# Decoded magnitudes kept in PSUM, and the second unit's key products and inverse started earlier, in a delta-rule attention and mixture-of-experts kernel

## The chip, the cores and the metric

The kernel runs on one core of a Trainium2 chip. The metric is the device time of one execution in microseconds, as the median of several runs. The engines are called by the names of the profile: PE (TensorE, matrix products), PEld (its weight loads), DVE (VectorE), ACT (ScalarE), POOL (GpSimd) and SP (SyncE, which issues most DMAs). All of them run in parallel, each through its own queue in order.

## The reference

Three parts follow one another. The change touches the first part and the preparation of the second.

```python
# 1: delta-rule attention, q, k, v of (4, 8, 768, 48), one state of 48 x 48 for each of 32 heads
k_n = k / (norm(k) + 1e-6)
for t in range(768):
    y[t] = q[t] @ state
    state = state + beta[t] * outer(k_n[t], v[t] - k_n[t] @ state)
# 2: x of (3072, 384) = the heads of y side by side; weights in float64
x = (((x @ w1) * (x @ w2)) @ w3) @ w_out
# 3: each of 3072 tokens goes through one of 8 experts, chosen by x @ w_gate + bias
out = gate * (relu(x @ e_w1[e]) @ e_w2[e])
```

## The kernel before

**Attention.** The 768 steps are cut into 12 chunks of 64 (`s`), and two chunks make a unit (`u`). Within a chunk the recursion is replaced by products with the inverse of a triangular matrix. For a unit, `gram` multiplies the keys with themselves on PE (four calls of 8 head pairs) and ACT copies the negated result from PSUM into `An`, one full copy and two small ones that bring the lower diagonal blocks of 32 together. `inverse` is a generator: it transposes these blocks so that all 32 x 128 small matrices lie across partitions (`Ab`), takes the norms from their diagonals (square root on ACT, then about ten short DVE operations), scales `Ab` by beta and the norms, runs 31 rows of a recursion (two DVE operations each, `tmp` and `Tt`), multiplies with beta and transposes back (`An`, `TT`). Each `next` on the generator is one step. `merge1` and `merge2` join the blocks of 32 to 64 (products `pe`, `pf`, copies on ACT). Then follows the chain of a chunk: `chain_k` (values scaled with the norms by `scaled`, on POOL, less what the state says), `chain_u` (product with the inverse, `pu`), `chain_y` (the output, `py`, put by DMA into the token layout `x`), `chain_s` (the new state, `pS`). `masked` multiplies queries with keys.

**Start-up.** `startup` reads the float64 weights as raw words, 36 tiles in the order of `todo`: 8 tiles of w_out (384 columns), 16 of w3 and 12 of w1 and w2 (512 columns). A tile is decoded by two ACT operations, the magnitude (`mag`) and the low part, and two DVE operations that join them. Raw tiles go to ten buffers; `mag` alternates between two buffers in SBUF, which lie with the tenth raw buffer in the tile `spare` under the name `An1`. `sc`, in the place of the second unit's `TT`, takes the decoded tile. w_out is transposed and multiplied with the gate weights (`wot`, `wog`); w3 is folded with w_out on PE (`pw`) and split into two parts (`w34h`, `w34l`); w1 and w2 are only split (`w`).

**Order.** The wrapper `Engine` records each operation and makes every engine execute in the order of the program text, so all lines of the profile are its line 84, and groups are told apart by tile names. The order in start-up is written out by hand: `tick(n)` issues ACT's decode of tile n + 1, DVE's of tile n, what has become due (`flush`), new raw loads, and PE's use of tile n; the table `do` hangs other work behind a tick. `FC` is 8, so `FC + 3` is tick 11. In `do` stand the steps of the first inverse (`EARLY`, `START0`: four steps behind each of ticks 8 to 15), the chain of chunk 0 (from tick 17, one function for each tick), the key products of unit 1 (`GRAMS`, ticks 19 to 22), the routing set-up and the first steps of the second inverse (`WORK1`, ticks 30 to 33). After tick 33 the first token block follows: `moe1` runs 12 blocks of 256 tokens with 8 slices `f` each; a slice multiplies with w1 and w2 (`pAB`, two PSUM buffers of the name `AB`), DVE forms the product `a`, ACT and DVE split it (`ch`, `cl`), and `second` multiplies with the folded weights (`px`). `slot` places the attention of the following chunk between the slices, and `PLAN1` says how many steps of the second inverse the first block takes behind each slice. Tiles 34 and 35 are decoded within slices 0 and 1 of the first block (`rest`).

Of the kernel before, what the change touches and what calls it, by code (L numbers as in the profile page):

```python
# [53 lines left out]
MID = (0,) * 5 + (0, 0, 1) + (2, 2, 2, 1, 1, 1, 1, 2)  # L54
PLAN1 = (3, 4, 4, 4, 5, 4, 4, 2)
WORK1 = (1, 1, 1, 1)
AHEAD, W0 = 8, 0
CHAIN, GRAMS = (1, 1, 1, 1, 1, 1), (2, 3, 4, 5)
START0 = (4, 4, 4, 4, 4, 4, 4, 4, 2)

REST = (1, 1)
EARLY = (4, 2)
LEAD = 1
# [40 lines left out]
class Kernel:  # L104
# [162 lines left out]

    def keys(self, u):

        nc, a2 = self.nc, self.a2  # L270
        kT = a2.tile([P, NU, C], F32, tag="kT", name="kT")
        for c in range(US):
            nc.sync.dma_start(out=kT[:, c * NP:(c + 1) * NP].rearrange("p n t -> p (n t)"), in_=self.k_t[u * US + c])
        bt = a2.tile([P, 32], F32, tag="bt", name="bt")
        nc.sync.dma_start(out=bt, in_=self.beta[u])
        self.st[u] = dict(kT=kT, bt=bt)
# [10 lines left out]
    def gram(self, u, a):  # L287

        nc, a1, ps = self.nc, self.a1, self.ps
        st = self.st[u]
        if "An" not in st:
            st["An"] = a1.tile([P, NU, C], F32, tag=f"An{(u + 1) % 2 if u else 0}", name="An")
        An, kT = st["An"], st["kT"]
        pg = ps.tile([P, HP, C], F32, tag="ps", name="pg")
        for n in range(HP):
            for h in range(2):
                o, w = (1 - h) * C, h * C  # L300
                nc.tensor.matmul(pg[o:o + C, n], kT[w:w + C, a + n], kT[w:w + C, a + n], start=True, stop=True)
        yield
        nc.scalar.activation(An[:, a:a + HP], pg, AF.Copy, scale=-1.0)

        for h in range(2):
            o = h * C + 32
            nc.scalar.activation(An[o:o + 32, a:a + HP, 0:32], pg[o:o + 32, :, 32:64], AF.Copy, scale=-1.0)
# [9 lines left out]
    def scaled(self, s):  # L317
        u, c = divmod(s, US)
        vt = self.st["v", s]
        self.nc.gpsimd.tensor_tensor(out=vt, in0=vt, in1=self.st[u]["r"][:, c * NP:(c + 1) * NP].unsqueeze(2).to_broadcast([P, NP, D]), op=ALU.mult)  # L320

    def inverse(self, u):
# [6 lines left out]
        nc.gpsimd.memset(T, 0.0)  # L329
        nc.gpsimd.memset(T.rearrange("p a b -> p (a b)")[:, 0:1024:33], 1.0)  # L330
        nc.vector.transpose(Ab.rearrange("n j i -> n i j"), An[:, :, 0:32].rearrange("j n i -> j i n"))

        ss, r, r2, rb = (a2.tile([P, 32], F32, tag=x, name=x) for x in ("ss", "r", "r2", "rb"))
        nc.vector.tensor_scalar(out=ss, in0=Ab.rearrange("p a b -> p (a b)")[:, 0:1024:33], scalar1=-1.0, scalar2=0.0, op0=ALU.mult, op1=ALU.max)
        nc.scalar.activation(r, ss, AF.Sqrt)
        yield
# [10 lines left out]
        st["r"] = rb  # L347
        nc.vector.tensor_tensor(out=Ab, in0=Ab, in1=bt.unsqueeze(2).to_broadcast([P, 32, 32]), op=ALU.mult)
        yield
        tmp = a1.tile([P, 256], F32, tag="tmp", name="tmp")  # L350
        for j in range(31):
# [5 lines left out]
            yield  # L357
        nc.vector.tensor_tensor(out=T, in0=T, in1=bt.unsqueeze(1).to_broadcast([P, 32, 32]), op=ALU.mult)

        nc.vector.transpose(An[:, :, 0:32].rearrange("i n c -> i c n"), T)  # L360
# [161 lines left out]
    def startup(self):  # L522
# [3 lines left out]
        nc, pm, wp, m1 = self.nc, self.pm, self.wp, self.m1  # L526
        self.keys(0)

        self.w12 = [[[[None] * KC for _ in range(2)] for _ in range(2)] for _ in range(2)]
# [3 lines left out]
        sc = self.TT[1].rearrange("p n c -> p (n c)").rearrange("p (a b) -> p a b", b=DCH)  # L533
        spare = self.a1.tile([P, 4, DCH], F32, tag="An1", name="spare")
        ms = [spare[:, x] for x in range(2)]
        wg = self.cp.tile([P, KC, E], F32, tag="wg", name="wg")
# [18 lines left out]
        def issue():  # L555
            while issued[0] < len(todo):
                n = issued[0]
# [12 lines left out]
                if kind != "o":  # L570
                    out[n] = sc[:, n % 4]
                mag[n] = ms[n % 2][:, :src.shape[-1]]
                tag = usable[0]
                free.remove(tag)
                k = src.shape[-1]
                t = spare[:, 2:4].rearrange("p a b -> p (a b)")[:, 0:2 * k].bitcast(I64) if tag == "raw" else (wp if tag[0] == "w" else m1).tile([P, k], I64, tag=tag, name="raw")
                nc.sync.dma_start(out=t, in_=src)
# [3 lines left out]
        def scalar(n):  # L581

            if n < len(todo):
                L, Hw, _ = raw[n]

                nc.scalar.activation(mag[n], Hw.bitcast(F32), AF.Abs, scale=2.0 ** -112)
# [58 lines left out]
        def tick(n):  # L645
            self.n = n
            scalar(n + 1)
            vector(n)
# [4 lines left out]
        def split(g):  # L653

            next(g)
            after.append((self.n + 1, lambda: list(g)))

        inv = self.inverse(0)
        prep = lambda a: self.prep(0, [a * HP])
        step = lambda: next(inv, None)  # L660
        do = {-1: [lambda: prep(0), lambda: prep(1), lambda: scalar(0), lambda: prep(2), lambda: prep(3)], 1: [step],
              FC - 4: [lambda: self.queries(0), lambda: self.values(0), self.routing_loads], 
              FC + 3: [lambda: split(self.masked(0))], FC + 5: [lambda: self.tokens(0), lambda: self.keys(1), lambda: self.values(1)]}

        for x in EARLY:
            do.setdefault(FC - x, []).append(step)
        GAPS = list(CHAIN)
# [8 lines left out]
        for x in range(0, NU, HP):  # L676
            do.setdefault(FC + len(START0) + GRAMS[x // HP], []).append(lambda x=x: split(self.gram(1, x)))
        do.setdefault(t, []).append(lambda: setattr(self, "work", self.inverse(1)))
        for n, k in enumerate(WORK1, NSTART - len(WORK1)):
            do.setdefault(n, []).extend([lambda: next(self.work)] * k)  # L680
# [5 lines left out]
        issue()  # L686
        nc.sync.dma_start(out=wg, in_=self.w_gate.rearrange("(k p) e -> p k e", p=P))
        for n in range(-1, NSTART):
# [122 lines left out]
    def routing_setup(self):  # L811
# [526 lines left out]
```

## Time and profile before

| | us |
|---|---|
| median of 3 runs | 858.41 (857.83 to 858.80) |
| the profiled execution | 855.77 |
| its span, first to last instruction | 854.0 |
| PE busy | 796.9 (93%) |
| DVE busy | 613.7 (72%) |
| ACT busy | 409.6 (48%) |
| POOL busy | 162.7 (19%) |

The busy shares are means over the whole span. The start-up and the first token block, which the change rearranges, take the first 196 us or so and have limits of their own; they are read from windows and from the timeline. In a row of the timeline stand the start, the duration, the engine, the line, the operation, the tile that is written and those that are read, how many instructions were merged, and in brackets how long the engine had been idle and what ended that.

### The profile page before, as it was taken

Reading aid. Unit: us, or ns where it says so; the run is one execution under the profiler, and the core shown is the slowest. Engines: PE = TensorE matmul, PEld = TensorE weight load, DVE = VectorE, ACT = ScalarE, POOL = GpSimd, SP = SyncE. Lnnn points to the kernel's source line nnn. Section 1 sums busy time; section 2 is a strip of 40 time slices with the busy share of each in tenths; the row PEclk is TensorE's granted clock in tenths of the full one; section 3 lists DMA queues with packets and bytes.
Section 4 is the critical chain, followed back from the end, with each engine's and each line's share of the span. In section 5 each row is a group of like instructions: output and inputs, shape, how many; then the busy total and the mean of one; then the engine's idle time right before and its main releaser. Section 6 shows DMA issues by size and latency. Waiting matters only on the chain.

```text
span 854.0 us, 24817 instructions
## 1 busy us (share of the span) xinstructions
PE 796.9 (93%) x10223; PEld 739.6 (87%) x10223; DVE 613.7 (72%) x1512; ACT 409.6 (48%) x863; POOL 162.7 (19%) x174
## 2 busy tenths in 40 slices
PE   3977879989999999999999999999899999999994
PEld 3844638988999999999999999999899999999983
DVE  3897399969866986698669874457786678667651
ACT  6525964462445344624462444335555565655541
POOL 5000300010001000100010000003244564545420
PEclk8588979999999999999999999999999999999998
DMA  9835434303220322032202121028457768667620
GB/s 301 289 102 186 126 98 135 83 17 85 71 82 6 98 71 83 21 87 80 68 26 78 39 64 40 2 90 264 128 157 247 243 229 267 227 211 249 223 63 6
DMA packets 48777, 105.42 MB, mean 123 GB/s; under 512 B 9412, under 2 KB 28756, under 8 KB 48656
## 3 DMA queue, kind: packets, MB, share of 16 engines
q1 hardware_dynamic: 41424, 88.35, 33.5%
q0 software_dynamic: 4064, 11.06, 3.8%
q10 hardware_dynamic: 3168, 4.34, 1.4%
q8 instruction: 82, 1.34, 0.7%
q14 instruction: 39, 0.32, 0.1%
HBM read 89.15 MB, written 10.63 MB: 117 GB/s over the span
## 4 chain that ended last, share of the span: by engine, by line
PE 62%; DVE 8%; issue 8%; POOL 4%; ACT 1%; DMA 1%; SPq 0%; POOLq 0%; ACTq 0%; DVEq 0%
PE pAB L84 23%; PE px L84 14%; PE ph L84 7%; PE spy L84 4%; PE py L84 2%; PE pq L84 2%; PE pk L84 2%; PE pu L84 2%; PE pS L84 2%; POOL w1l L84 2%; PE pg L84 1%; PE pe L84 1%; DVE Tt L84 1%; POOL out_dram L84 1%; DVE tmp L84 1%
## 5 line engine op out<-in xcount | busy, mean ns | idle before, releaser
L84 PE MATMUL pAB<-x,w 128*128 128x256 f32 x1728 | 231.3, 288 | 0.0
L84 PEld LDWEIGHTS pAB<-x,w 128*128 128x128 f32 x1728 | 214.6, 192 | 4.1
L84 ACT CAST ch<-a 128x256 fp32r<-128x256 f32 x96 | 38.9, 406 | 117.7 <-DVE a L84 117.7
L84 ACT COPY a<-pAB 128x256 f32<-128x256 f32 x96 | 35.7, 372 | 124.5 <-PE pAB L84 118.4
L84 DVE TENSOR_TENSOR a<-a,pAB 128x256 f32<-128x256 f32 x96 | 39.9, 416 | 73.6 <-ACT a L84 73.4
L84 PE MATMUL ph<-sxh,w1h 128*128 128x256 f32 x288 | 82.1, 285 | 0.5 <-DVE hl L84 0.5
L84 PE MATMUL ph<-sxh,w1l 128*128 128x256 f32 x288 | 80.8, 281 | 0.0
L84 PE MATMUL ph<-sxl,w1h 128*128 128x256 f32 x288 | 80.8, 280 | 0.0
L84 ACT ACTIVATE hh<-ph 128x256 fp32r<-128x256 f32 x96 | 37.0, 385 | 89.1 <-PE ph L84 88.7
L84 DVE TENSOR_TENSOR Tt<-tmp,Tt 128x31 f32<-128x31 f32 (+15 forms) x186 | 63.8, 343 | 6.6 <-DVE tmp L84 0.2
L84 DVE SCALAR_TENSOR_TENSOR hl<-ph,hh 128x256 fp32r<-128x256 f32 x96 | 40.2, 419 | 39.0 <-ACT hh L84 37.7
L84 DVE TENSOR_TENSOR w2l<-r,w2h 128x768 fp32r<-128x768 f32 x56 | 59.3, 1071 | 12.3 <-ACT w2h L84 12.1
L84 DVE TENSOR_TENSOR tmp<-Ab,Tt 128x31 f32<-128x31 f32 (+15 forms) x186 | 65.4, 352 | 3.2
L84 PE MATMUL px<-w34h,ch 128*128 128x392 f32 x192 | 65.8, 343 | 0.8 <-DVE w34l L84 0.8
L84 PE MATMUL px<-w34h,cl 128*128 128x392 f32 x192 | 65.3, 340 | 0.0
L84 PE MATMUL px<-w34l,ch 128*128 128x392 f32 x192 | 65.2, 339 | 0.0
L84 POOL TENSOR_TENSOR w1l<-r,w1h 128x512 fp32r<-128x512 f32 x39 | 50.5, 1313 | 50.4 <-ACT w1h L84 50.2
L84 POOL TENSOR_TENSOR vt<-vt,rb 128x768 f32<-128x768 f32 x12 | 18.2, 1519 | 201.6 <-DMA vt<-in_v_dram 117.7
L84 PEld LDWEIGHTS ph<-sxh,w1h 128*128 128x128 f32 x288 | 54.3, 188 | 1.3 <-DVE hl L84 1.1
L84 PE MATMUL pw<-wosW,TT 128*128 128x392 f32 x80 | 37.0, 605 | 19.5 <-DVE TT L84 19.2
L84 DVE TENSOR_TENSOR cl<-a,ch 128x256 fp32r<-128x256 f32 x96 | 40.4, 421 | 19.6 <-ACT ch L84 18.8
L84 PEld LDWEIGHTS ph<-sxh,w1l 128*128 128x128 f32 x288 | 54.3, 189 | 0.0
(262 smaller groups left out, 1742.9 us busy)
## 6 DMA issues: line engine op xcount, KB each, us to landing
r<-in_e_w_dram SPq DMA_DIRECT2D x42, 512.0 KB, 4.7
r<-in_e_w_dram SPq DMA_DIRECT2D x56, 384.0 KB, 3.9
raw<-in_w_dram SPq DMA_DIRECT2D x25, 512.0 KB, 4.8
kT<-in_kt_dram SPq DMA_DIRECT2D x12, 512.0 KB, 4.1
W<-in_q_dram SPq DMA_DIRECT2D x24, 256.0 KB, 4.4
vt<-in_v_dram SPq DMA_DIRECT2D x12, 384.0 KB, 4.6
kb<-in_kb_dram SPq DMA_DIRECT2D x12, 384.0 KB, 3.5
x2d<-xr ACTq DMA_DIRECT2D x22, 192.5 KB, 3.0
```

Source lines behind the costliest of these rows:

```text
L84: x = f(*a, **kw)
```

## The change

The magnitudes move from SBUF to PSUM: for tiles 0 to 9 to the buffers of the name `pc`, for tiles 10 to 34 to the two of the name `AB`, for tile 35 to a quarter of `sc`. The tile `spare` and with it the tenth raw buffer are gone, and `An1` is free for the second unit. The key products of unit 0 go to four PSUM buffers, all ahead of the first tile; their full copies run on DVE behind ticks 0 to 2, the small ones stay on ACT. The first w_out tile is loaded between the two halves of the first keys, the second behind them, and the gate weights follow. The steps of the first inverse begin behind tick 2 and end behind tick 14, where they ended behind tick 16; the chain begins behind tick 15, where it began behind tick 17. Beta is put on the diagonal of T at the outset, so the product of T with beta at the end falls away. The keys of unit 1 are loaded behind tick 6 instead of 13, their products run behind ticks 9, 10, 12 and 13, and 16 steps of the second inverse behind ticks 16 to 21; the first block takes the other 21. The first two units have one more step, since the square root is a step of its own. The first values are scaled on DVE. The routing set-up moves from ticks 9 to 11 behind ticks 16 to 18, with its PSUM tile in `ps`. Of the tiles of w1 and w2, one now follows each of the last eight tiles of w3, and four come last.

```diff
-PLAN1 = (3, 4, 4, 4, 5, 4, 4, 2)
-WORK1 = (1, 1, 1, 1)
+PLAN1 = (3, 4, 4, 3, 3, 2, 1, 1)
+WORK1 = {0: 2, 1: 2, 2: 3, 3: 3, 4: 3, 5: 3}
-CHAIN, GRAMS = (1, 1, 1, 1, 1, 1), (2, 3, 4, 5)
-START0 = (4, 4, 4, 4, 4, 4, 4, 4, 2)
+CHAIN, GRAMS = (1, 1, 1, 1, 1, 1), (-6, -5, -3, -2)
+START0 = (3, 3, 3, 3, 3, 3, 3)
-EARLY = (4, 2)
+EARLY = {2: 1, 3: 1, 4: 2, 5: 4, 6: 4, 7: 4}
...
     def keys(self, u, also=lambda: None):
             nc.sync.dma_start(out=kT[:, c * NP:(c + 1) * NP]..., in_=self.k_t[u * US + c])
+            if c == 0:
+                also()
...
     def gram(self, u, a):
-            st["An"] = a1.tile([P, NU, C], F32, tag=f"An{(u + 1) % 2 if u else 0}", name="An")
+            st["An"] = a1.tile([P, NU, C], F32, tag=f"An{u % 2}", name="An")
-        pg = ps.tile([P, HP, C], F32, tag="ps", name="pg")
+        own = {2: "x0", 3: "AB"}.get(a // HP) if u == 0 else None
+        pg = self.pm.tile([P, HP, C], F32, tag=own, ...) if own else ps.tile([P, HP, C], F32, tag="ps", name="pg")
...
-        nc.scalar.activation(An[:, a:a + HP], pg, AF.Copy, scale=-1.0)
+        if u == 0:
+            nc.vector.tensor_scalar(out=An[:, a:a + HP], in0=pg, scalar1=-1.0, scalar2=None, op0=ALU.mult)
+        else:
+            nc.scalar.activation(An[:, a:a + HP], pg, AF.Copy, scale=-1.0)
...
     def scaled(self, s):
-        self.nc.gpsimd.tensor_tensor(out=vt, in0=vt, in1=..., op=ALU.mult)
+        (self.nc.gpsimd if s else self.nc.vector).tensor_tensor(out=vt, in0=vt, in1=..., op=ALU.mult)
...
     def inverse(self, u):
-        nc.gpsimd.memset(T.rearrange("p a b -> p (a b)")[:, 0:1024:33], 1.0)
...
+        if u < 2:
+            yield
         nc.scalar.activation(r, ss, AF.Sqrt)
...
-        nc.vector.tensor_tensor(out=Ab, in0=Ab, in1=bt.unsqueeze(2).to_broadcast([P, 32, 32]), op=ALU.mult)
+        nc.vector.tensor_tensor(out=Ab, in0=Ab, in1=bt.unsqueeze(1).to_broadcast([P, 32, 32]), op=ALU.mult)
+        nc.vector.tensor_copy(T.rearrange("p a b -> p (a b)")[:, 0:1024:33], bt)
...
-        nc.vector.tensor_tensor(out=T, in0=T, in1=bt.unsqueeze(1).to_broadcast([P, 32, 32]), op=ALU.mult)
...
     def startup(self):
-            k = (x + 1 - AHEAD) * (len(w12) - sum(REST)) // (K3 - AHEAD)
+            k = x + 1 - AHEAD
-        free = [f"w{m}1{kk}" for kk in range(KC) for m in range(2)] + ["x0", "x1", "xr", "raw"]
+        free = [f"w{m}1{kk}" for kk in range(KC) for m in range(2)] + ["x0", "x1", "xr"]
...
+                if n < FC + 2:
+                    mag[n] = self.pc.tile([P, DCH], F32, tag="pc", name="mag")
+                elif n <= NSTART:
+                    mag[n] = pm.tile([P, DCH], F32, tag="AB", name="mag", bufs=2)
+                else:
+                    mag[n] = sc[:, (n + 2) % 4]
...
         def tick(n):
+            if n >= NSTART:
+                flush(n)
...
+        self.keys(0, lambda: issue(1))
+        issue(2)
+        nc.sync.dma_start(out=wg, ...)
+        issue()
+        grams = [self.gram(0, a) for a in range(0, NU, HP)]
+        for g in grams:
+            next(g)
+        do = {-1: [lambda: scalar(0)], 0: [lambda: list(grams[0])], 1: [lambda: list(grams[1]), lambda: list(grams[2])], 2: [lambda: list(grams[3])],
+              FC - 2: [lambda: self.keys(1)], ...
-        do.setdefault(t, []).append(lambda: setattr(self, "work", self.inverse(1)))
-        for n, k in enumerate(WORK1, NSTART - len(WORK1)):
+        c = FC + len(START0)
+        do.setdefault(c + 1, []).append(lambda: setattr(self, "work", self.inverse(1)))
+        for n, k in WORK1.items():
...
-            do.setdefault(FC + 1 + x, []).append(lambda: next(rs, None))
+            do.setdefault(FC + 8 + x, []).append(lambda: next(rs, None))
...
-        pmod = self.pm.tile([P, NTILE], F32, tag="AB", name="pmod", bufs=2)
+        pmod = self.ps.tile([P, NTILE], F32, tag="ps", name="pmod")
```

## Rows read from the trace of the kernel before

**Rows 1.** Windows: busy us of PE, PEld, DVE, ACT, POOL; PEclk, DMA, GB/s

```profile
0.00:15.60 15.60, 7.22 (x131) 6.88 (x131) 2.14 (x4) 9.71 (x20) 12.61 (x33) 0.95 0.88 297
15.60:74.30 58.70, 44.22 (x198) 30.33 (x198) 54.13 (x120) 23.15 (x47) 1.84 (x1) 0.72 0.67 216
74.30:110.00 35.70, 27.42 (x609) 20.46 (x610) 17.71 (x29) 31.99 (x59) 6.56 (x11) 0.90 0.40 116
110.00:130.00 20.00, 17.05 (x102) 9.62 (x101) 18.96 (x36) 12.29 (x23) 0.00 (x0) 0.84 0.44 136
130.00:196.00 66.00, 61.48 (x1106) 57.83 (x1105) 56.45 (x137) 32.95 (x69) 6.03 (x6) 0.97 0.24 67
```

**Rows 2.** Timeline of DVE: the first transpose

```profile
15.61 2.10 DVE L84 STREAM_TRANSPOSE Ab<-An 128x1024 f32<-128x1024 f32 x1
```

**Rows 3.** Timeline of DVE and POOL from 33 to 75 us

```profile
33.55 2.56 DVE L84 SCALAR_TENSOR_TENSOR TT<-spare,TT 128x512 int32<-128x512 int32 x2
...
33.73 1.84 POOL L84 TENSOR_TENSOR vt<-vt,rb 128x768 f32<-128x768 f32 x1 [19.73 <-DVE Tt L84]
...
69.59 1.23 DVE L84 TENSOR_TENSOR Tt<-Tt,bt 128x1024 f32<-128x1024 f32 x1
...
74.34 0.66 DVE L84 SCALAR_TENSOR_TENSOR TT<-spare,TT 128x512 int32<-128x512 int32 x1
```

**Rows 4.** Windows of DVE alone: norm and scaling, twelve recursion rows, routing

```profile
21.50:24.80 3.30, 3.06 (x11) 0.50 1.03 407
31.30:33.50 2.20, 1.96 (x9) 0.50 1.02 325
36.00:38.90 2.90, 2.66 (x9) 0.50 0.83 299
40.40:43.78 3.38, 3.14 (x9) 0.86 0.50 153
49.10:50.53 1.43, 1.33 (x7) 1.00 0.00 0
```

**Rows 5.** Timeline: ACT, copies of a key product; DVE, tiles 25, 30, 33

```profile
104.16 1.39 ACT L84 ACTIVATE An<-pg 128x512 f32<-128x512 f32 x3
...
107.94 0.68 DVE L84 SCALAR_TENSOR_TENSOR TT<-spare,TT 128x512 int32<-128x512 int32 x1
...
117.72 0.68 DVE L84 SCALAR_TENSOR_TENSOR TT<-spare,TT 128x512 int32<-128x512 int32 x1
...
129.17 0.68 DVE L84 SCALAR_TENSOR_TENSOR TT<-spare,TT 128x512 int32<-128x512 int32 x1
```

**Rows 6.** Timeline of PE, first block; last a window with the clock

```profile
129.27 4.58 PE L84 MATMUL pAB<-x,w 128*128 128x256 f32 x36
...
175.28 2.21 PE L84 MATMUL pe<-An 32*32 32x32 f32 x128 [2.55 <-DVE An L84]
...
177.42 3.86 PE L84 MATMUL pAB<-x,w 128*128 128x256 f32 x18
...
179.50:181.20 1.70, 1.70 (x10) 1.70 (x9) 0.00 (x0) 1.68 (x2) 1.64 (x3) 0.50 0.00 0
```

**Rows 7.** Groups of instructions: busy us, mean ns of one, idle before

```profile
L84 ACT ACTIVATE spare<-raw 128x512 f32<-128x512 f32 x18 | 12.2, 678 | 17.9 <-issue 9.0 <-DVE TT L84 8.8
...
L84 ACT ACTIVATE An<-pg 32x256 f32<-32x256 f32 x16 | 6.0, 376 | 0.3
...
L84 ACT ACTIVATE An<-pg 128x512 f32<-128x512 f32 x8 | 4.8, 600 | 4.9 <-PE pg L84 4.8
...
L84 DVE SCALAR_TENSOR_TENSOR hl<-ph,hh 128x256 fp32r<-128x256 f32 x96 | 40.2, 419 | 39.0 <-ACT hh L84 37.7
...
L84 DVE TENSOR_TENSOR cl<-a,ch 128x256 fp32r<-128x256 f32 x96 | 40.4, 421 | 19.6 <-ACT ch L84 18.8
```

**Rows 8.** DMA issues: count, KB each, median us to landing

```profile
raw<-in_w_dram SPq DMA_DIRECT2D x25, 512.0 KB, 4.8
```

More of the change, by code (lines that the diff above doesn't have):

```diff
@@ L266, in attn_setup, with keys @@
         self.wos = ((big.rearrange("p (g n) -> p g n", n=XW), 5), (R, 1), (K, 1), (one, 1))
-    def keys(self, u):
+    def keys(self, u, also=lambda: None):
         nc, a2 = self.nc, self.a2
@@ L294, in gram @@
         if "An" not in st:
-            st["An"] = a1.tile([P, NU, C], F32, tag=f"An{(u + 1) % 2 if u else 0}", name="An")
+            st["An"] = a1.tile([P, NU, C], F32, tag=f"An{u % 2}", name="An")
         An, kT = st["An"], st["kT"]
-        pg = ps.tile([P, HP, C], F32, tag="ps", name="pg")
+        own = {2: "x0", 3: "AB"}.get(a // HP) if u == 0 else None
+        pg = self.pm.tile([P, HP, C], F32, tag=own, name="pg", bufs=2 if own == "AB" else 1) if own else ps.tile([P, HP, C], F32, tag="ps", name="pg")
         for n in range(HP):
@@ L319, in scaled @@
         vt = self.st["v", s]
-        self.nc.gpsimd.tensor_tensor(out=vt, in0=vt, in1=self.st[u]["r"][:, c * NP:(c + 1) * NP].unsqueeze(2).to_broadcast([P, NP, D]), op=ALU.mult)
+        (self.nc.gpsimd if s else self.nc.vector).tensor_tensor(out=vt, in0=vt, in1=self.st[u]["r"][:, c * NP:(c + 1) * NP].unsqueeze(2).to_broadcast([P, NP, D]), op=ALU.mult)
     def inverse(self, u):
@@ L526, in startup @@
         nc, pm, wp, m1 = self.nc, self.pm, self.wp, self.m1
-        self.keys(0)
         self.w12 = [[[[None] * KC for _ in range(2)] for _ in range(2)] for _ in range(2)]
@@ L533, in startup @@
         sc = self.TT[1].rearrange("p n c -> p (n c)").rearrange("p (a b) -> p a b", b=DCH)
-        spare = self.a1.tile([P, 4, DCH], F32, tag="An1", name="spare")
-        ms = [spare[:, x] for x in range(2)]
         wg = self.cp.tile([P, KC, E], F32, tag="wg", name="wg")
@@ L549, in startup, with issue @@
         last = {f"w{m}1{kk}": todo.index(("w", (m, 1, kk))) for kk in range(KC) for m in range(2)}
-        free = [f"w{m}1{kk}" for kk in range(KC) for m in range(2)] + ["x0", "x1", "xr", "raw"]
+        free = [f"w{m}1{kk}" for kk in range(KC) for m in range(2)] + ["x0", "x1", "xr"]
         raw, out, mag, after = {}, {}, {}, []
         issued = [0]
-        def issue():
-            while issued[0] < len(todo):
+        def issue(upto=100):
+            while issued[0] < min(upto, len(todo)):
                 n = issued[0]
@@ L571, in issue @@
                     out[n] = sc[:, n % 4]
-                mag[n] = ms[n % 2][:, :src.shape[-1]]
                 tag = usable[0]
@@ L575, in issue @@
                 k = src.shape[-1]
-                t = spare[:, 2:4].rearrange("p a b -> p (a b)")[:, 0:2 * k].bitcast(I64) if tag == "raw" else (wp if tag[0] == "w" else m1).tile([P, k], I64, tag=tag, name="raw")
+                t = (wp if tag[0] == "w" else m1).tile([P, k], I64, tag=tag, name="raw")
                 nc.sync.dma_start(out=t, in_=src)
@@ L584, in scalar @@
                 L, Hw, _ = raw[n]
+                if n < FC + 2:
[4 more added lines that the diff above has]
+                    mag[n] = sc[:, (n + 2) % 4]
+                mag[n] = mag[n][:, :L.shape[-1]]
                 nc.scalar.activation(mag[n], Hw.bitcast(F32), AF.Abs, scale=2.0 ** -112)
@@ L656, in split @@
             after.append((self.n + 1, lambda: list(g)))
+        self.keys(0, lambda: issue(1))
+        issue(2)
+        nc.sync.dma_start(out=wg, in_=self.w_gate.rearrange("(k p) e -> p k e", p=P))
+        issue()
         inv = self.inverse(0)
@@ L660, in startup @@
         step = lambda: next(inv, None)
-        do = {-1: [lambda: prep(0), lambda: prep(1), lambda: scalar(0), lambda: prep(2), lambda: prep(3)], 1: [step],
+        grams = [self.gram(0, a) for a in range(0, NU, HP)]
+        for g in grams:
+            next(g)
+        do = {-1: [lambda: scalar(0)], 0: [lambda: list(grams[0])], 1: [lambda: list(grams[1]), lambda: list(grams[2])], 2: [lambda: list(grams[3])],
               FC - 4: [lambda: self.queries(0), lambda: self.values(0), self.routing_loads],
-              FC + 3: [lambda: split(self.masked(0))], FC + 5: [lambda: self.tokens(0), lambda: self.keys(1), lambda: self.values(1)]}
-        for x in EARLY:
-            do.setdefault(FC - x, []).append(step)
+              FC - 2: [lambda: self.keys(1)],
+              FC + 3: [lambda: split(self.masked(0))], FC + 5: [lambda: self.tokens(0), lambda: self.values(1)]}
+        for x, k in EARLY.items():
+            do.setdefault(x, []).extend([step] * k)
         GAPS = list(CHAIN)
@@ L677, in startup @@
             do.setdefault(FC + len(START0) + GRAMS[x // HP], []).append(lambda x=x: split(self.gram(1, x)))
-        do.setdefault(t, []).append(lambda: setattr(self, "work", self.inverse(1)))
-        for n, k in enumerate(WORK1, NSTART - len(WORK1)):
-            do.setdefault(n, []).extend([lambda: next(self.work)] * k)
+        c = FC + len(START0)
+        do.setdefault(c + 1, []).append(lambda: setattr(self, "work", self.inverse(1)))
+        for n, k in WORK1.items():
+            do.setdefault(c + 1 + n, []).extend([lambda: next(self.work)] * k)
         rs = self.routing_setup()
         for x in range(3):
-            do.setdefault(FC + 1 + x, []).append(lambda: next(rs, None))
+            do.setdefault(FC + 8 + x, []).append(lambda: next(rs, None))
         do.setdefault(t + 3, []).append(lambda: self.parts_x(0))
         do.setdefault(NSTART - 1, []).extend([lambda: self.tokens(1), lambda: self.tokens(2)])
-        issue()
-        nc.sync.dma_start(out=wg, in_=self.w_gate.rearrange("(k p) e -> p k e", p=P))
         for n in range(-1, NSTART):
```

## The prediction

> **What bounds the kernel now.** I read the stages first, from the table of windows [rows 1]. Five stretches matter, and what stands in front of each number is which engine is nearly full. Up to 15.6 us VectorE (DVE) is busy 2.14 us: it waits for the first tile. From 15.6 to 74.3 us it is busy 54.1 of 58.7 us, so DVE is the bound: it decodes tiles 0 to 15 and runs the first unit's inverse. From 74.3 to 110 us ScalarE (ACT) is busy 32.0 of 35.7 us and DVE only 17.7: here the first chunk's chain (merge, u, y, state) passes from TensorE (PE) to ACT and back, ACT also decodes and copies the second unit's key products, and 18 us of DVE lie idle. From 110 to 130 us DVE is full again (19.0 of 20). From 130 to 196 us, the first token block, PE is busy 61.5 of 66 us and DVE 56.5: PE is the bound, and it loses 4.5 us to DVE. After that PE is the bound to the far end and the change touches little. So the change is worth what it takes out of the DVE-bound stretches, and what it puts into the 18 idle us without lengthening the chain. I follow four marks: DVE's start of tile 16, of tile 22 and of tile 33, and PE's second product of the first block.
>
> **Up to tile 16 (before: 74.34 us [rows 3]).** Key products of unit 0 now go to four PSUM buffers at once; their large copies move from ACT to DVE. The trace has no such copy on DVE; a DVE operation of 512 columns takes 0.68 us [rows 5], the same copy on ACT 0.60 [rows 7], so 0.6 to 0.7 each, 2.8 us for four, all in a stretch where DVE is idle for 13 of 15.6 us. ACT is rid of four copies of 0.6 us before the first transpose, and the first w_out tile is asked for ahead of the second half of the keys, at some 1.2 us; with a landing like the median of the big loads, 4.8 us [rows 8], it is there at 6. From then ACT's queue up to the transpose holds four tiles (two operations of 384 columns each, 0.55 by columns from the 0.678 for 512 [rows 7]), eight small copies of 0.376 [rows 7] and one of about 0.5: 7.9 us. With some 1.2 us of waits on DVE between, I put the transpose at 15.1 us against 15.61 [rows 2], but with tile 2 already decoded (1.2, two DVE operations of 384 columns). Gain 1.7.
> The product with beta over the whole T (1.23 us [rows 3]) goes; in its place comes a copy of 32 columns, 0.25 with its gap. Gain 1.0. The scaling of the first values leaves POOL: beside its 1.84 us two decode operations took 2.56 us instead of 1.36 [rows 3, 5]. Gain 1.2. [...] The routing set-up, 1.4 us of DVE [rows 4], is only moved behind tile 16: 1.5 here, given back below. DVE idles 4.6 us in this stretch [rows 1]; 1.6 of it are single waits on ACT early on, which a DVE with more to do per tile does not have. Sum: 1.7 + 1.0 + 1.2 + 1.5 + 1.6 = 7.0, so tile 16 starts at about **67.3 us**.
>
> **Magnitudes in PSUM** change no count. That ACT writes PSUM is not in the trace; its magnitude costs 0.678 us from SBUF to SBUF, a copy of as many columns out of PSUM 0.600 [rows 7], so I bound it by 0.08 either way, 34 times: up to 2.7 us, of ACT, which has slack except beside the chain; I take 0. For DVE, the operation hl, with one operand in PSUM, took 0.419 us and cl, with both in SBUF, 0.421 [rows 7]: no price, and I take 0. [...] One raw buffer fewer: loads run 9 tiles ahead, not 10, and tiles 34 and 35 are asked for only after tiles 30 and 31. Four tiles at the pace below are 7.8 us and a load lands in 4.8 [rows 8], so I take 0; if loads crowd and land twice as late, tile 34 is 1.8 us late, the upper end. The second keys move ahead on SP's queue, to tile 6: the raw loads behind them are late by their 1 MB, some 3 us at the 300 GB/s of the first stretch [rows 1], against a lead of 8 tiles; nothing.
>
> **Tile 16 to tile 22.** This is where the idle DVE is used. Its work now: six tiles at 1.35, 8.1 (two operations each [rows 5]); two low parts of w1/w2 and one of the fold, 1.7; the routing, 1.5; the scaling of the first values, by columns from the 1.23 us for 1024 [rows 3], 0.95; and 16 steps of the second inverse: transpose and norm input 2.3 [rows 2], norm and scaling 3.3, and 13 rows of the recursion, the first 0.4 and the next twelve 2.2 + 2.9 + 3.4 = 8.5 [rows 4], in all 14.7 with the diagonal. Together 27.0. The key products of unit 1 (four times 1.39 us of ACT [rows 5]) are out of this stretch, beside the fold, where ACT is busy 23 of 58.7 us [rows 1]. Chain and DVE run side by side, with one wait that I can place: in tile 18 the low part of a w1 tile waits for ACT's high part, which stands behind the copies of the second merge on ACT's queue, about 2.9 us. So tile 22 starts near 67.3 + 27.0 + 2.9 = **97.2**, with 14.7 us of the second inverse behind it.
>
> **Tile 22 to tile 33 (before: 129.17 [rows 5]).** No inverse step and no key product is left here. The pace of such tiles stands in the trace: from 107.94 (tile 25) to 117.72 us five tiles with their splits, 1.96 each [rows 5]. (Tile 25, at 107.94 before, comes near 103.) Eleven make 21.5; POOL's scaling of the second values now falls on a busy DVE, 1.2 as above. Tile 33 starts at **119.9**, 9.3 earlier.
>
> **The first block.** The last two PSUM magnitudes sit in the two buffers of pAB. The first product waits for tile 33, which is about done. The second waits for DVE to read tile 34's magnitude, and before that DVE has tile 33 (1.35), two low parts (1.3), R (1.1), a, a row of the recursion and cl (0.4 + 0.9 + 0.4), a fold part (0.5) and the read itself (0.7): 6.6, so 126.5. Queued behind it on PE are u, the masked queries and every later product. Before, the second product began at 129.27 + 2.29 = 131.56 [rows 6]. Lead **5.1**. From here PE is the bound. It lost 4.5 us [rows 1], of which 2.55 were one wait for the second inverse [rows 6], which now ends inside the block; 0.9 belong to the routing and stay. Gain 3.6. After that wait one product took 3.86 us instead of 2.29, with the granted clock at 0.50, the lower of its two levels [rows 6]; this goes (1.5), but PE now idles some 4 us ahead of the second product and should pay the same there. Sum: 5.1 + 3.6 = **8.7 us**. The profiled execution (855.8 us, span 854.0) would become 847.1; it lies 2.6 below the median of the runs, 858.4, so I forecast 849.7.
>
> **Rivals.** *More is saved (845.3).* If DVE does not stand still in tile 18 (2.9) and PE's clock holds through the short wait (1.5), the gain is 8.7 + 4.4 = 13.1. For it: ACT loses 5.6 us of work there; against it: 32.0 of 35.7 us.
> *PSUM reads are dear (852.4).* If a decode operation on DVE pays for PSUM the 0.08 us by which ACT's two rows differ, the only gap between the memories that the rows show [rows 7], 34 tiles cost 2.7 us, all in stretches that DVE bounds: 8.7 less 2.7 is 6.0. Against it: hl and cl. [...]
> *The work only moves (857.4).* If idle DVE time is not filled but displaced, what is left is what DVE no longer does: twice 1.0 and the 1.2 of the collision, less 0.95 for the scaling and 1.2 for the new collision, 1.0 in all. Against it: the 18 us are idle because ACT and PE are the bound there.
> *The chain is strung out (slower, 861.7).* Each tile's chain step on PE stands behind that tile's fold, which needs DVE; DVE's next split needs ACT; ACT's copies need PE. If, instead of running side by side, the 14.7 us of inverse between tiles 16 and 22 are met by such waits one after another, most of them, 12 us, come on top of the 8.7 saved: 3.3 slower. It decides against the change from the point where tile 22 starts later than about 106 us.
>
> **How the numbers follow.** Forecast, 846 to 853: 0.60. More saved: 0.14. PSUM dear: 0.10. Only moved: 0.08. Strung out: 0.08. Range 844.5 to 856: it takes in the first three with their bounds and leaves out the last two. A difference of 0.2% (1.7 us) is about what a measurement of this kernel can tell from none. Faster 0.84, same 0.08, slower 0.08.
>
> **What will show it.** In the new trace: the transpose of unit 0 near 15 us; tile 16 near 67 and the first merge's products near 71; tile 22 near 97 with the twelfth row of the second recursion done; DVE idle between 74 and 110 us down from 18 to under 6; decode operations still 0.68; the second pAB product behind a wait of 3 to 4 us; no wait of 2.55 before the second unit's merge. I am wrong if a decode operation takes over 0.72 us, if tile 22 begins after 100, or if PE's wait before the second product exceeds 6 us.

## The result, and the profile after

The changed kernel takes **849.51 us** (median; 848.02 to 850.87) against 858.12 (857.06 to 858.80) for the kernel before in the same comparison: a ratio of 0.990, 95% interval 0.9881 to 0.992, or 8.6 us less. The forecast was 849.7. The profiled execution of the changed kernel took 850.87 us, its span 849.2.

The same five windows as [rows 1], now of the changed kernel (us, busy PE, PEld, DVE, ACT, POOL, then granted clock, DMA share, GB/s):

```profile
0.00:15.60 15.60, 7.49 (x141) 7.19 (x142) 5.95 (x11) 8.98 (x19) 10.76 (x22) 1.00 0.89 284
15.60:74.30 58.70, 48.95 (x453) 33.94 (x452) 52.92 (x116) 31.87 (x64) 2.42 (x11) 0.80 0.62 210
74.30:110.00 35.70, 24.24 (x353) 15.75 (x352) 31.72 (x71) 22.30 (x42) 5.51 (x9) 0.81 0.42 130
110.00:130.00 20.00, 15.99 (x122) 10.97 (x121) 18.34 (x32) 14.55 (x28) 0.00 (x0) 0.96 0.63 175
130.00:196.00 66.00, 65.11 (x1238) 61.48 (x1237) 49.50 (x129) 32.41 (x67) 5.83 (x5) 0.99 0.21 61
```

DVE works 3.8 us more ahead of 15.6 us. Between 74.3 and 110 it idles 4.0 us where it idled 18.0. Between 130 and 196 PE loses 0.9 us where it lost 4.5, but its wait of 2.6 us ahead of the second product now lies before 130. The marks on DVE, from its timeline, with POOL's scaling of the second values, which answer to [rows 2, 3, 5]:

```profile
15.31 2.13 DVE L84 STREAM_TRANSPOSE Ab<-An 128x1024 f32<-128x1024 f32 x1 [1.59 <-ACT An L84]
...
69.62 0.57 DVE L84 TENSOR_TENSOR w34l<-pw,w34h 128x392 fp32r<-128x392 f32 x1 [2.76 <-ACT w34h L84]
70.10 0.68 DVE L84 SCALAR_TENSOR_TENSOR TT<-mag,TT 128x512 int32<-128x512 int32 x1
...
92.62 0.69 DVE L84 TENSOR_TENSOR w<-TT,w 128x512 fp32r<-128x512 f32 x1 [2.04 <-ACT w L84]
...
96.88 2.27 DVE L84 TENSOR_TENSOR tmp<-Ab,Tt 128x231 f32<-128x231 f32 x1
97.39 1.49 POOL L84 TENSOR_TENSOR vt<-vt,rb 128x768 f32<-128x768 f32 x1
99.18 0.40 DVE L84 TENSOR_TENSOR Tt<-tmp,Tt 128x231 f32<-128x231 f32 x1
...
101.28 0.68 DVE L84 SCALAR_TENSOR_TENSOR TT<-mag,TT 128x512 int32<-128x512 int32 x1
...
121.87 0.69 DVE L84 SCALAR_TENSOR_TENSOR TT<-mag,TT 128x512 int32<-128x512 int32 x1
```

Tile 16 starts at 70.10 us (before 74.34), tile 22 at 101.28, tile 33 at 121.87 (before 129.17). On PE the first products and the second unit's merge, which answer to [rows 6]:

```profile
122.70 2.39 PE L84 MATMUL pAB<-x,w 128*128 128x256 f32 x18
127.71 3.59 PE L84 MATMUL pAB<-x,w 128*128 128x256 f32 x18 [2.62 <-DVE a L84]
...
168.52 2.21 PE L84 MATMUL pe<-An 32*32 32x32 f32 x128
170.67 2.42 PE L84 MATMUL pAB<-x,w 128*128 128x256 f32 x18
```

The window of the second pAB product, with the clock:

```profile
127.70:131.20 3.50, 3.49 (x18) 3.29 (x18) 3.36 (x8) 1.56 (x3) 0.00 (x0) 0.61 1.02 226
```

The lead over before is 3.85 us at the second pAB product (131.56 before), 6.8 at `pe`, with no wait ahead of it, and 8.2 at the routing product `pr` (187.74 against 195.97). There it stays until some 600 us. Two later marks on PE, `spt`, first of the changed kernel, then of the kernel before:

```profile
600.07 0.44 PE L84 MATMUL spt<-ident,xg 128*128 128x128 f32 x2 [1.15 <-DVE sxl L84]
...
662.95 0.38 PE L84 MATMUL spt<-ident,xg 128*128 128x128 f32 x2
```
```profile
608.05 0.44 PE L84 MATMUL spt<-ident,xg 128*128 128x128 f32 x2 [1.15 <-DVE sxl L84]
...
667.88 0.38 PE L84 MATMUL spt<-ident,xg 128*128 128x128 f32 x2
```

At the first the lead is 8.0 us, at the second 4.9, and the two profiled spans differ by 4.8. So the missing 3 us lie between these marks, in the clock: PE does the same work there in 59.0 busy us after the change, at a mean clock of 0.95, and in 56.1 before, at 1.00, and idles 3.9 and 3.7 us. First a window of the changed kernel, then of the kernel before:

```profile
600.00:620.00 20.00, 17.93 (x114) 17.63 (x115) 15.47 (x44) 6.92 (x15) 4.24 (x5) 0.91 0.52 163
```
```profile
600.00:620.00 20.00, 16.39 (x121) 15.78 (x119) 15.80 (x45) 10.67 (x26) 5.50 (x6) 1.00 0.46 129
```

The changed kernel's clock drops to 0.50 twice (from 606.4 to 609.6 us and from 640.6 to 643.8), that of the kernel before stays at 1.00. Of the profiled executions of kernels with a part of the change, all but one (*PSUM only*, 1.00) had a mean of 0.94 to 0.97 between 600 and 660 us, whatever they gained; the profiled execution of the kernel before, with 1.00, lay 2.6 below its own median. So the experiments are compared by their marks up to 196 us, and behind that mainly by the medians.

### The profile page after: what moved, and what is told of

Same layout as the page of the kernel before. It is cut to its first block, busy times and chain, and to the rows that moved or that the text cites. A ratio compares the mean times of both kernels' runs of the same rounds, so it can differ in the third digit from the quotient of the medians.

```text
span 849.2 us, 24808 instructions
## 1 busy us (share of the span) xinstructions
PE 796.1 (94%) x10223; PEld 739.2 (87%) x10223; DVE 610.1 (72%) x1517; ACT 407.1 (48%) x859; POOL 160.8 (19%) x167
## 4 chain that ended last, share of the span: by engine, by line
PE 67%; DVE 12%; issue 9%; POOL 4%; ACT 4%; DMA 3%; SPq 0%; POOLq 0%; ACTq 0%; DVEq 0%
PE pAB L84 23%; PE px L84 13%; PE ph L84 7%; PE spy L84 4%; PE py L84 3%; PE pu L84 3%; PE pq L84 2%; PE pk L84 2%; PE pg L84 2%; PE pw L84 2%; DVE TT L84 2%; PE pS L84 2%; POOL w1l L84 2%; PE pe L84 1%; POOL out_dram L84 1%
## 5 line engine op out<-in xcount | busy, mean ns | idle before, releaser
L84 DVE TENSOR_TENSOR tmp<-Ab,Tt 128x31 f32<-128x31 f32 (+15 forms) x186 | 67.1, 361 | 3.0
L84 PEld LDWEIGHTS ph<-sxl,w1h 128*128 128x128 f32 x288 | 54.9, 191 | 0.0
L84 ACT CAST w1h<-r 128x512 fp32r<-128x512 f32 x84 | 49.4, 616 | 2.3 <-DMA r<-in_e_w_dram 1.9
```

What stands on the lines that cost most here:

```text
L84: x = f(*a, **kw)
```

## The experiments

Marks of each trace (us; `pAB` is the first product of the first block), and the median with its difference from the kernel before on the same chip. The names are those of the sections below. The kernel before had a median of 857.94 us beside *late inverse*, *late inverse and products*, *PSUM only* and *copies later*, 857.70 beside *chain two later*, *early steps alone*, *keys first* and *pAB free*, and 858.73 beside the last four.

| kernel | first `pAB` | `pe`, unit 1 | `pr` | median | to before |
|---|---|---|---|---|---|
| before | 129.27 | 175.28 | 195.97 | 858.12 | |
| changed | 122.70 | 168.52 | 187.74 | 849.51 | -8.6 |
| late inverse | 121.41 | 165.86 | 186.53 | 848.28 | -9.7 |
| late inverse and products | 121.50 | 167.53 | 187.92 | 848.44 | -9.5 |
| PSUM only | 130.61 | 176.67 | 197.30 | 856.61 | -1.3 |
| copies later | 122.92 | 168.48 | 187.70 | 848.73 | -9.2 |
| chain two later | 124.38 | 170.05 | 189.26 | 849.22 | -8.5 |
| early steps alone | 127.47 | 173.50 | 195.30 | 856.54 | -1.2 |
| keys first | 124.78 | 170.38 | 189.60 | 849.20 | -8.5 |
| pAB free | 123.74 | 168.28 | 187.50 | 848.88 | -8.8 |
| less DVE work | 125.59 | 170.49 | 191.17 | 853.78 | -5.0 |
| early start | 126.33 | 172.38 | 194.29 | 855.50 | -3.2 |
| both | 123.81 | 168.57 | 189.26 | 850.91 | -7.8 |
| late inverse, pAB free | 115.49 | 166.23 | 186.98 | 847.03 | -11.7 |

### Is it the early second inverse?

*Late inverse*, the changed kernel with

```diff
-PLAN1 = (3, 4, 4, 3, 3, 2, 1, 1)
-WORK1 = {0: 2, 1: 2, 2: 3, 3: 3, 4: 3, 5: 3}
+PLAN1 = (3, 4, 4, 4, 5, 4, 5, 2)
+WORK1 = {14: 1, 15: 1, 16: 1, 17: 1}
...
-        do.setdefault(c + 1, []).append(lambda: setattr(self, "work", self.inverse(1)))
+        do.setdefault(c + 7, []).append(lambda: setattr(self, "work", self.inverse(1)))
```

> The changed kernel with the second unit's inverse put back to where it was: one step behind each of ticks 30 to 33, the rest in the first block; its key products stay early. Theory A (what pays is that the inverse fills DVE's idle time beside the chain): the first block is DVE-bound again and the kernel takes 853.5 us or more, against 849.5. Rival B (the early inverse holds the chain up by about as much as it takes out of the first block; the gain lies in the ACT work and the DVE work taken away): tile 22 starts 8 us or more ahead of 101.28, tile 33 4 to 6 ahead of 121.87, and the kernel takes 848 to 851 us.

*Late inverse and products*, the same with the key products of unit 1 late again:

```diff
-GRAMS = (-6, -5, -3, -2)
+GRAMS = (2, 3, 4, 5)
```

> As e1_late_inverse, and the key products of the second unit too are back beside the chain (two to five ticks behind its start). What is left of the change is the earlier start, the magnitudes in PSUM, the missing product with beta, the values on DVE and the tile order. Theory A: the products alone are worth little, e2 within 1.5 us of e1. Rival B: ACT is the bound beside the chain, so the 5.6 us of their copies come back there: 3 to 5.6 us more than e1, 852 to 855.

Measured: 848.28 us, ratio 0.987 (0.9845 to 0.9895), and 848.44, ratio 0.9898 (0.9875 to 0.9922). Neither median is above the changed kernel's. With the late inverse tile 22 came at 90.79 us, 10.5 ahead of the changed kernel, as rival B said, but tile 33 only 1.3 ahead, where it had 4 to 6. What the early inverse does is seen from windows between the first transpose and tile 33; first the kernel before, then the changed one, then the one with the late inverse:

```profile
15.60:129.17 113.57, 87.85 (x902) 59.63 (x902) 90.00 (x181) 66.59 (x127) 8.39 (x12) 0.80 0.54 170
```
```profile
15.30:121.87 106.57, 84.09 (x879) 55.87 (x880) 96.60 (x205) 64.51 (x122) 7.93 (x20) 0.82 0.53 171
```
```profile
15.30:120.58 105.28, 85.19 (x897) 56.65 (x896) 86.85 (x179) 66.44 (x126) 6.41 (x10) 0.82 0.56 183
```

The changed kernel puts 9.75 us more of DVE work (96.60 less 86.85) ahead of tile 33 and takes only 1.29 us longer to get there; DVE's idle time falls from 18.4 to 10.0. The idle time is filled, as intended, but the work came from a place where it cost next to nothing. PE's timeline with the late inverse, at the second merge:

```profile
165.86 2.21 PE L84 MATMUL pe<-An 32*32 32x32 f32 x128 [0.37 <-DVE An L84]
168.00 2.41 PE L84 MATMUL pAB<-x,w 128*128 128x256 f32 x18
```

With 31 steps of the inverse in the first block instead of 21, DVE is 0.37 us late for the merge, and the merge itself is 2.7 us earlier than in the changed kernel; at `pr` 1.2 of this are left, behind a wait of 2.35 us for DVE. With the key products late as well, `pr` comes 1.4 us later than with the late inverse alone, which the medians (848.44 against 848.28) do not show. Rival B of the second run, 852 to 855 us, falls. So the early inverse does not carry the gain, and the early key products carry at most 1.7 us of it in the traces (at `pe`) and none in the medians.

### Is it the place of the chain, or PSUM?

*Chain two later*, the changed kernel with `START0 = (3, 3, 3, 2, 2, 2, 2, 2, 2)`, so that the chain begins behind tick 17 again:

> The changed kernel, but the last 21 steps of the first inverse are spread over nine tiles again instead of seven, so that the first chunk's chain (merge, u, y, state) begins two tiles later, as before the change; nothing else differs, the same work is done. Theory A: the gain comes from the place of the chain. In the changed kernel pe starts at 69.74 us against 80.12, and the stretch behind it is a ping-pong of PE, ACT and DVE of a nearly fixed length. Two tiles (1.35 us each, and a low part of 0.56) put pe 3.3 us later; the chain then ends 3.3 later and so does tile 33: 852 to 853.5, pe of the first unit at 72.5 to 74. Theory B: DVE is the bound of the whole way to tile 33 (it idles only 4.0 of 35.7 us behind 74.3), so the order in which its work is done decides nothing: 848.5 to 850, tile 33 within 1 us of 121.87.

*Early steps alone*, the kernel before with the first inverse two tiles earlier:

```diff
-START0 = (4, 4, 4, 4, 4, 4, 4, 4, 2)
+START0 = (3, 3, 3, 3, 3, 3, 3)
-EARLY = (4, 2)
+EARLY = {3: 1, 4: 2, 5: 4, 6: 4, 7: 4}
```

> The kernel before, with one part of the change alone: the steps of the first inverse begin beside tiles 3 to 7 (1, 2, 4, 4 and 4 steps) and go on with three a tile, so that the chain begins two tiles earlier. Loads, key products, the product with beta, POOL's scaling and the second inverse stay as they were. Theory A (the place of the chain gives the gain): pe, which stood at 80.12, comes 3.3 us earlier, two tiles of 1.35 and a low part of 0.56, and the marks behind it follow: 854 to 855.5, about 3.3 us below the kernel before. Theory B (only the work taken off DVE and its earlier start gain): 857 to 859, with tile 33 within 1 us of 129.17.

Measured: 849.22 us, ratio 0.9901 (0.9868 to 0.9934), and 856.54, ratio 0.9992 (0.9972 to 1.0011). The chain's place is worth 1.5 to 1.8 us at the first block in both traces, yet not more than 1.2 in either median. Theory A, which had 3.3 us, falls. Theory B has the time of the first run, but not its mark (tile 33 at 123.55 us, 1.7 later than in the changed kernel), and the second run lies between the two theories.

*PSUM only*, the kernel before with the magnitudes in PSUM as in the change (`pc` and `AB`, and the routing's `pmod` in `ps`; the tenth raw buffer stays):

> The kernel before with one part of the change alone: the magnitudes in PSUM, in the same buffers as in the change, and the routing's small transpose in another PSUM buffer to make room. Theory: DVE pays nothing for PSUM (decode operations stay at 0.68 to 0.69 us); the only effect is that the first block's second product waits, since the last magnitudes hold a buffer of it: 0 to 2 us slower than before. Rival (PSUM is dear): decode operations of 0.74 us or more, 2 to 3 us slower.

Measured: 856.61 us, ratio 0.9987 (0.9971 to 1.0004): no price in the median, though the marks of its trace are 1.3 to 1.4 us later than before, with a wait of 2.25 us for DVE ahead of the first `pAB`. The theory names such a wait, at the second product. The groups by form up to 135 us, of the changed kernel:

```profile
L84 DVE SCALAR_TENSOR_TENSOR TT<-raw,TT 128x512 int32<-128x512 int32 x28 | 19.4, 692 | 1.0
L84 DVE SCALAR_TENSOR_TENSOR TT<-mag,TT 128x512 int32<-128x512 int32 x27 | 18.4, 682 | 0.0
L84 ACT ACTIVATE mag<-raw 128x512 f32<-128x512 f32 x27 | 17.4, 644 | 12.0 <-DVE TT L84 5.8 <-DVE wos L84 2.4 <-DVE wosK L84 1.9
...
L84 ACT ACTIVATE mag<-raw 128x384 f32<-128x384 f32 x8 | 4.1, 510 | 8.9 <-DMA raw<-in_w_out_dram 5.6 <-DVE wosR L84 3.3
```

The DVE operation fed from PSUM takes 682 ns, its neighbour with both inputs in SBUF 692; in the kernel with PSUM only the first takes 683 (x26).

### What carries it: less work on DVE, and an early start

*Less DVE work*, the kernel before with this alone:

```diff
-        nc.gpsimd.memset(T.rearrange("p a b -> p (a b)")[:, 0:1024:33], 1.0)
...
-        nc.vector.tensor_tensor(out=Ab, in0=Ab, in1=bt.unsqueeze(2)..., op=ALU.mult)
+        nc.vector.tensor_tensor(out=Ab, in0=Ab, in1=bt.unsqueeze(1)..., op=ALU.mult)
+        nc.vector.tensor_copy(T.rearrange("p a b -> p (a b)")[:, 0:1024:33], bt)
...
-        nc.vector.tensor_tensor(out=T, in0=T, in1=bt.unsqueeze(1)..., op=ALU.mult)
...
-        self.nc.gpsimd.tensor_tensor(out=vt, in0=vt, ...)
+        (self.nc.gpsimd if s else self.nc.vector).tensor_tensor(out=vt, in0=vt, ...)
```

> The kernel before, with one part of the change alone: the product of T with beta goes (beta stands on the diagonal at the start of the recursion), and the first values are scaled on DVE and not on POOL. Theory B (DVE is the bound not only to tile 33 but up to the second unit's merge at 175.28 us, where PE waits 2.55 us for it): the first product with beta gives 1.0, the collision 1.2 less 0.95 for the scaling, and the second product with beta another 1.0 ahead of the second merge. Together 2.25: some 855.5 (854.7 to 856.3), with the product pe of the second unit at 173. Theory C (the gain of the change comes from its early start and from ordering alone): 857 to 858.5.

Measured: 853.78 us, ratio 0.9943 (0.9925 to 0.996): 4.95 us, twice what theory B said. Where the rest comes from is seen on PE ahead of the first merge. The kernel before, timeline and then window:

```profile
75.78 4.42 PE L84 MATMUL pw<-wosW,TT 128*128 128x392 f32 x8 [4.63 <-DVE TT L84]
80.12 2.21 PE L84 MATMUL pe<-An 32*32 32x32 f32 x128
```
```profile
75.80:80.10 4.30, 4.30 (x8) 2.20 (x8) 3.04 (x6) 4.04 (x7) 0.00 (x0) 0.64 0.41 121
```

The kernel with less DVE work, timeline (with two marks of DVE and the second merge) and then window:

```profile
32.45 1.41 DVE L84 SCALAR_TENSOR_TENSOR TT<-spare,TT 128x512 int32<-128x512 int32 x2
...
72.17 0.65 DVE L84 SCALAR_TENSOR_TENSOR TT<-spare,TT 128x512 int32<-128x512 int32 x1
...
73.60 2.90 PE L84 MATMUL pw<-wosW,TT 128*128 128x392 f32 x8 [3.39 <-DVE TT L84]
76.43 2.21 PE L84 MATMUL pe<-An 32*32 32x32 f32 x128
...
170.49 2.21 PE L84 MATMUL pe<-An 32*32 32x32 f32 x128 [1.35 <-DVE An L84]
172.63 2.41 PE L84 MATMUL pAB<-x,w 128*128 128x256 f32 x18
```
```profile
73.60:76.40 2.80, 2.80 (x8) 1.44 (x8) 1.56 (x3) 2.77 (x5) 0.00 (x0) 1.00 0.19 41
```

Tile 16 comes at 72.17 us, 2.17 earlier: 1.23 for the product with beta and 1.15 for the collision (1.41 instead of 2.56), less the 0.2 of the copy of beta. Before, PE came out of a wait of 4.63 us with the clock at 0.64, and the eight fold products that stand ahead of the merge took 4.42 us; now they take 2.90 with the clock at 1.00. 2.17 and 1.52 are 3.69; `pe` leads by 3.69 and the first pAB product by 3.68. The second product with beta takes 1.20 off the wait at `pe` (2.55 to 1.35): 4.8. The scaling (0.95, at 79.82 us) falls into a wait for ACT, of which 0.61 are left behind it, and costs nothing. The product behind the second merge is shorter too (2.41 us; before 3.86, with the clock at 0.56), but `pr` then waits 2.37 us for DVE where it waited 0.89, so that this last gain is given back.

*Early start*, the kernel before with the load order, the four PSUM buffers and DVE copies of the first key products, and `START0` and `EARLY` of the change:

> The kernel before, with one part of the change alone: the first w_out tile is loaded ahead of the second half of the keys and the gate's weights behind the second tile, the first key products lie in four PSUM buffers, their large copies are made by DVE, and the first inverse begins beside tiles 2 to 7. All else (product with beta, POOL's scaling, magnitudes in SBUF, tile order, second key products and inverse) stays. Theory B: two tiles more, 1.15 us each, are decoded by the first transpose, and the earlier steps give the 1.8 us by which the first pAB product led in the run with early steps alone; 4.1 in all: 853 to 854.5. Theory D (what is gained ahead of the first block is lost at the second unit's merge, as in that run, whose lead of 1.8 had shrunk to 0.7 behind it): 856 to 857.5, with the lead at pe of the second unit at least 2 us above the lead behind it.

Measured: 855.50 us, ratio 0.9964 (0.9951 to 0.9977), between the two theories. By the first transpose DVE has decoded one tile more than before (three instead of two), not two more as theory B has it. On PE:

```profile
172.38 3.62 PE L84 MATMUL pe<-An 32*32 32x32 f32 x128 [2.57 <-DVE An L84]
175.93 3.67 PE L84 MATMUL pAB<-x,w 128*128 128x256 f32 x18
```

The lead is 2.9 us up to `pe`, and PE waits as long there as before (2.57 against 2.55); behind it `pe` takes 3.62 us instead of 2.21, and of the lead 1.7 are left at `pr`. So theory D has the direction and not the size: the lead goes on to the end of the stretch that DVE bounds, and there 1.2 us of it, where the theory has at least 2, are lost to the longer `pe`; the mean clock from 130 to 196 us was 0.95 (before 0.97).

*Both*, the kernel before with these two edits:

> The kernel before with the two parts above together, and without the rest of the change: magnitudes in SBUF, old tile order, old routing set-up, second key products and second inverse as late as before. Theory B: the parts add, 4.1 + 2.25 = 6.35 us, and most of the wait of 2.55 at the second merge goes too, since DVE comes to it earlier than PE: 849.5 to 851.5. Theory E (the rest of the change, the tile order or the routing above all, carries a share of over 2 us): 852 to 855.

Measured: 850.91 us, ratio 0.9912 (0.9896 to 0.9929): 7.8 us, where 5.0 and 3.2 add to 8.2. Theory B holds, though half of the wait at the second merge stays (1.33 us). The rest of the change is worth at most 1.4 us in the medians, and the intervals of the ratios overlap; in the traces it is 1.5 us at `pr` and 2.6 at the `spt` near 600 us (602.64 against 600.07). So the rest is small, but not shown to be nothing. The move of the routing and the order of the tiles were not tried alone.

### Smaller points

*Keys first*, the changed kernel with `self.keys(0)` ahead of every w_out tile:

> The changed kernel with the two loads of the first keys asked for ahead of every w_out tile, as before the change; all else stays. DVE, which decodes two tiles ahead of its first transpose at 15.31 us, gets the first tile later. Theory 1 (the early start is a term of the gain): the decode of tiles 0 and 1, 1.2 us of DVE each, falls behind the transpose, tile 16 and all marks behind are later by 1.2 to 2.4: 850.5 to 852. Theory 2 (DVE has idle time enough on the way to tile 16, 58.7 less 52.9 us): within 0.7 of the changed kernel, 848 to 850.

Measured: 849.20 us, ratio 0.9906 (0.9874 to 0.9939). All marks are 1.9 to 2.1 us later, as theory 1 says, but the median stays, as theory 2 says. The same holds for the chain two later. A lead of under 2 us at `pr` is not told from none by these medians. In the profiled executions it is lost between the two `spt` marks: this stretch takes 62.9 us in the changed kernel, 59.5 with the keys first (from 601.51 us) and 61.4 with the chain two later (from 601.11), at mean clocks, between 600 and 660 us, of 0.94, 0.97 and 0.97. Whether it is so in every execution stays open.

*Copies later*, the changed kernel with the last step of the first inverse, which makes ACT's two copies of `TT`, one tick later (`START0` ending in 2, `EARLY` with `15: 1`):

> The changed kernel with the last step of the first inverse (two ACT copies, 2.1 us) one tick later, so that ACT's high part of the fold no longer stands behind it. Theory: DVE's wait of 2.76 us ahead of tile 16 shrinks to under 1 and tile 16 starts 2 us earlier, at 68; DVE being the bound to the first block, 847.5 to 848.5 us. Rival: another wait takes its place beside the chain and tile 22 starts at 101 as before; 849.5.

Measured: 848.73 us, ratio 0.9888 (0.9872 to 0.9905). Tile 16 comes at 68.83 instead of 70.10, and DVE does not wait ahead of it, but tile 22 starts at 101.60, as the rival says, and at the first pAB product nothing is left (122.92 against 122.70).

*pAB free*, the changed kernel with

```diff
-                elif n <= NSTART:
+                elif n < NSTART - 1:
...
-            if n >= NSTART:
+            if n >= NSTART - 2:
                 flush(n)
```

> The changed kernel with the magnitudes of tiles 33 and 34 in SBUF, so that the last two no longer sit in the two buffers of the pAB products. Theory 1: the 2.62 us that PE waits ahead of its second pAB product, and the 1.2 us that this product takes more at the lower clock, come from there; both go: second product near 125, 846 to 847.5. Theory 2: the wait only changes its name, since DVE, with tile 33, R and the slice a in its queue, hands over its next result at the same time: the second product stays at 127 to 128 and the time at 848.5 to 850.

Measured: 848.88 us, ratio 0.9901 (0.9862 to 0.994). PE's timeline:

```profile
123.74 4.57 PE L84 MATMUL pAB<-x,w 128*128 128x256 f32 x36
128.76 2.07 PE L84 MATMUL pu<-R,TT 64*64 64x48 f32 x64 [0.45 <-DVE R L84]
```

The first two products now follow each other without a wait, in 4.57 us, as before the change (4.58, with the clock at 1.00); but what comes behind them needs DVE, and the fifth product begins at 143.63 us against 143.87. Theory 2 holds for the time, not for the place: the wait goes elsewhere.

*Late inverse, pAB free*, both edits in one:

> The changed kernel with the second inverse begun as late as before the change, and with the magnitudes of tiles 33 and 34 in SBUF instead of the two buffers of the pAB products: a version that may beat both. With the late inverse alone, pe of the second unit came at 165.86 against 168.52, and the median lay 1.2 below the changed kernel's; without the wait ahead of the second pAB product up to 2 us more can go. If both add: 845.5 to 847.5. If DVE, which has the second inverse in the first block, is what the block waits for: 848 to 849.5.

Measured: 847.03 us (844.39 to 849.65), ratio 0.9857 (0.9835 to 0.9878), the lowest median of all kernels here, below each run of the changed one, though from another set of runs. Its marks are those of the late inverse (`pr` 186.98 against 186.53), and the wait stands again further on:

```profile
115.49 4.57 PE L84 MATMUL pAB<-x,w 128*128 128x256 f32 x36
125.30 3.33 PE L84 MATMUL pu<-R,TT 64*64 64x48 f32 x58 [5.25 <-DVE R L84]
```

So it is not shown that freeing the buffers gives anything beyond the late inverse, whose own runs reach from 844.75 to 850.40.

## Why the prediction was right, and where it was not

**The sum.** Forecast 8.7 us of lead behind the first block; measured 8.2 at `pr`, and 8.6 in the median.

**Up to tile 16** (forecast 67.3, measured 70.10). The transpose came at 15.31 (forecast 15.1) with three tiles decoded, tile 2 among them, as forecast. The term for small waits failed: the low part of the fold ahead of tile 16 waited 2.76 us for ACT's high part, which stands behind the two copies of `TT`, 2.11 us of ACT, on its queue (65.61 to 67.72 us). This wait is as long as the whole miss of 2.8 us. The kernel with the copies later shows that it cost nothing in the end.

**PSUM.** Taken at 0, and so it is; a decode operation took 0.68 us as before. ACT's magnitude became a little cheaper (644 ns for 678, 510 for 546) [rows 7]. DVE's decode operation fed from PSUM took 682 ns, its neighbour with both inputs in SBUF 692: no price shows. With that the rival *PSUM reads are dear* falls. The raw buffer that went has the price that stood at the upper end: ACT waited 1.75 us for tile 34's load.

**Tile 16 to tile 22** (forecast 27.0 and 2.9, measured 31.2). The wait for ACT was there, in tile 20 and of 2.0 us. The collision with POOL's scaling of the second values, which I had put behind tile 22, came at 96.88 us and cost 1.87 instead of 1.2 (`tmp` 2.27 for some 0.40): `tmp` ended 0.27 us behind POOL's 1.49 us, and `Tt` right after it took 0.40 again. Tile 22 came after 100, which I had named as a sign that I am wrong; it was 4.1 late, and behind it I was 2.1 too dear (20.6 us to tile 33, forecast 22.7).

**The first block.** Second product at 127.71 (forecast 126.5) behind a wait of 2.62 (forecast 3 to 4), with the clock at 0.61 for the product behind it, which took 3.59 us (forecast 1.5 more than 2.29): the cost was right. The releaser was not: it was `a` of the first slice, not DVE's read of tile 34's magnitude, which came only at 128.69 after its late load. From there the lead grew by 4.4 (forecast 3.6).

**Where the reason failed.** "This is where the idle DVE is used" describes the changed kernel and is not why it is faster. I took idle time of DVE between 74 and 110 us for time that can be sold. The step that failed is that I did not ask what the second inverse costs where it stood: the run with the late inverse keeps 18.4 us of idle DVE ahead of tile 33 and waits 0.37 us at the second merge. The rival *the work only moves* saw this half, but priced what DVE no longer does at 1.0 us. It is worth 5.0, as the run with less DVE work shows, and the early start, worth 3.2 alone, was not in the rival at all. Three of its terms were mis-sized: the scaling (0.95) falls into idle time; the new collision (1.2) arises only where the second inverse runs early beside POOL; and the clock ahead of the first merge (1.52) was not in it, though the row of 4.42 us for eight products stood in the trace of before. The marks came out near because they were added up over whole stretches; their split by cause did not. That the median fell within 0.2 us of the forecast is in part luck: tile 22 was 4.1 late, the stretch behind it 2.1 shorter and the growth of the lead in the first block 0.8 larger than forecast, and these errors cancel for the most part.

**The other rivals.** *More is saved* came true in neither of its two terms: DVE waited (2.04 us in tile 20), and PE's clock fell (0.61 at the second product). *The chain is strung out* needed tile 22 later than 106 us.

## What to carry to other kernels

Idle time of an engine is worth only what the work that fills it costs where it stands now; undo the move alone before crediting it. Follow the bounding engine to the point where another one first waits for it (here DVE, from the first transpose to the second unit's merge at 175 us): here each operation on that way counted in full (1.23 and 1.20 us of the products with beta), and one in a wait counted nothing (0.95 of the scaling). And a wait of PE can have a second price in the products behind it: here eight products took 4.42 us at a clock of 0.64 behind a wait of 4.63, and 2.90 at 1.00 behind one of 3.39; look for products of the same shape with two durations.

## Of the hardware, not expected

The length of a wait alone did not say whether the clock falls. After 3.39 us the eight fold products ran at 1.00, after 4.63 at 0.64; at the second merge a wait of 2.57 was followed by a `pe` of 3.62 us, one of 2.55 by a `pe` of 2.21 at 1.00 and a product of 3.86 at 0.56, and one of 1.35 by a `pe` of 2.21 and a product of 2.41. No threshold follows from these.
